# Pooled attention and two expert layers on one core: moving the keys, the second attention tile and the first weights to other places in a hand-written order

## The chip, the core and the metric

The kernel runs on one core of a Trainium2 chip. The core has engines that each work through their own instructions in order and wait for one another through semaphores: TensorE (PE) multiplies and transposes into PSUM, its weight loads (PEld) running beside the multiplications; VectorE (DVE) and ScalarE (ACT) read PSUM and SBUF; GpSimd (POOL) reads SBUF; SyncE (SP) and the others issue DMAs. The metric is device time in microseconds, lower is better; times are medians of several runs.

## The reference

```python
# q, k, v: batch 8, heads 8, sequence 576, head size 64
k_p = k.reshape(B, H, 72, 8, D).mean(axis=3)
v_p = v.reshape(B, H, 72, 8, D).mean(axis=3)
scores = (1 / sqrt(D)) * q @ k_p^T                  # 576 x 72 per head
attn = exp(scores - max); attn /= sum + 1e-9
x = (attn @ v_p)                                    # -> 4608 tokens x 512
h = x @ w_in; x = max(0.01 * h, h) @ w_out          # 512 -> 2048 -> 512, float64 weights
logits = x @ w_gate; e = argmax(logits)             # 8 experts, one per token
out = softmax(logits)[e] * (max(x @ w1[e], 0) @ w2[e])   # 512 -> 1024 -> 512
```

Keys and values are averaged over groups of 8 positions. All products are done with numbers split into a high and a low part (three multiplications for one).

## The kernel before

**Stages.** The 4608 tokens are 36 tiles of 128, two tiles to a block of 256, so 18 blocks. The first expert layer runs in 288 *slots*. A slot (b, f) is one `g1(b, f)` (12 multiplications of 256 columns: 512 inputs to 128 hidden units) and, one or two slots later, one `g2(b, f)` (6 multiplications of 512 columns, back to 512 outputs). Slots 0 to 31 hold blocks 0 and 1, interleaved; from slot 32 on a block b has the 16 slots 16b to 16b + 15. After slot 287 comes the second expert layer, which gathers tokens by expert.

**What is hung on the slots.** `at(slot, fn, ...)` puts a call into a list for a slot. In each slot the order is: `g1`, the calls of the list in the order in which they were put there (`run_slot`, line 956), `g2`, then the split of the hidden units (`g_hi`, `g_lo`). `plan()` (line 893) puts the calls there: first all attention calls, then `att_av`, then the keys and values, then the preparation of the second layer's weights (`ps_load`, `ps_split`, `ps_store`), then routing (`logit`, `route_a` to `route_c`). So in one slot attention stands ahead of keys and values, and these ahead of the logits.

**Attention of a tile t** of block b is done in the slots of block b - 1, counted from s: `att_a` (s - 1: four PE transposes of the queries, ScalarE copies them out), `att_b` (s + 1: scores into two PSUM banks; DVE takes the max and subtracts it, into `pr`, once per bank), `att_e` (s + 2: exp), `att_n` (s + 3: sum and normalisation on DVE), `att_c` (s + 5: PE transposes into two banks; ScalarE copies the high part to `at_t` and then `rm_t`, DVE subtracts to get the low part, into `at_t` and `rm_t`). `att_av(b)`, in the last slot of block b - 1, multiplies with the values: operands `at_t`, `rm_t`, `vm` (the first 64 pooled values of each head) and `vr` (the other 8). Its result `x_t` is the input of block b's `g1`.

**Keys and values of batch nb** (2 to 7): seven pieces of raw data, in two buffers (`kv`): 0 to 3 keys, 4 and 5 values, 6 the rest of the values. `kv_load` is a DMA on SP's queue. `kv_pool` adds up groups of 8, in three DVE additions (and a POOL multiplication, line 294, for piece 6), two slots ahead of `kv_use` (one for the pieces 4 to 6). `kv_use` of 0 to 3 is one PE transpose (line 307) and two ScalarE copies to `kT`; of 4 and 5 copies and subtractions to `vm`; of 6 the same to `vr`. `kv_load(i + 2)` follows `kv_use(i)`, as it takes its buffer.

**The PSUM banks.** Every PE result of attention, keys and routing takes one of two banks, in turn; a new one waits until the one before last is read:

```python
banks = {"att": ["a0", "a1"], "h": ["h0", "h1"]}
...
def pt(kind):
    turn[kind] += 1
    return bank(banks[kind][turn[kind] % len(banks[kind])])
...
        if i < 4:                                        # kv_use
            p = pt("att")
            nc.tensor.transpose(p[:, 0:SP], t[:, 0, 256:384], ident[0:SP, 0:SP])
```

**The start.** Before slot 0 a list written out by hand does batch 0's keys and values (`kv_load0_k`, `kv_load0_v`), the attention of tiles 0 and 1, and the first weights. The first layer's weights come as float64; `w_load64` loads a piece of 0.5 MB (`load2` calls it twice: a piece of `w_in` and one of `w_out`), `w_conv1` turns it into float32 (two ScalarE steps, lines 459 and 460, then four DVE instructions, lines 461 to 470), `w_conv2` splits it into high and low. The pieces 1 to 15 of both are converted in the slots.

Of the kernel before, what the change touches and what calls it, by code (L numbers as in the profile page):

```python
# [21 lines left out]
def kernel(  # L22
# [25 lines left out]
    NF = DFF // P  # L48
# [59 lines left out]
    def sb(shape, dt, tag, bufs=1):  # L108
        return pool.tile(shape, dt, name=tag, tag=tag, bufs=bufs)
# [7 lines left out]
# [3 lines that stand above are left out]
# [4 lines left out]
    def act_copy(o, i, scale=1.0):  # L124
        nc.scalar.activation(o, i, AF.Copy, scale=scale)  # L125

    def sub(eng, o, a, b):
        eng.tensor_tensor(out=o, in0=a, in1=b, op=ALU.subtract)  # L128
# [85 lines left out]
    def kv_load0_v(nb):  # L214
        vt = sb([P, 6, 512], F32, "w13")
        for par in range(2):
            nc.sync.dma_start(
                out=vt[64 * par:64 * par + 64, 0:4],
                in_=v[nb, par:H:2, 0:512, :].rearrange("h (m r) d -> m h (r d)", r=POOL),
            )  # L220
        for h in range(H):
            nc.sync.dma_start(
                out=vt[8 * h:8 * h + 8, 4, :], in_=v[nb, h, 512:576, :].rearrange("(m r) d -> m (r d)", r=POOL)
            )
        kv_raw[nb, 4] = vt[:, 0:2]
        kv_raw[nb, 5] = vt[:, 2:4]
        kv_raw[nb, 6] = vt[0:64, 4:5]
        kv_raw[nb, 7] = vt[0:64, 5, :].rearrange("p (h d) -> p h d", h=H)
# [107 lines left out]
    def segs(c0, n):  # L336
        r, done = [], 0
        while done < n:
            b, s = divmod(c0 + done, S)
            w = min(n - done, S - s)  # L340
            r.append((done, w, b, s))
            done += w
        return r

    def q_load(t):
        x = q0[:, t] if t < 4 else sb([P, H, D], F32, "q")
        for o, n, b, s in segs(t * P, P):
            nc.sync.dma_start(out=x[o:o + n], in_=q[b, :, s:s + n, :].rearrange("h s d -> s h d"))
        q_sb[t] = x

    def att_a(t):
        x = q_sb.pop(t)
        p = pt("att")
        for pr in range(NPAIR):
            nc.tensor.transpose(p[:, pr * P:pr * P + P], x[:, 2 * pr:2 * pr + 2, :], ident)
        qT = alt[:, 0:512].rearrange("p (a n) -> p a n", a=NPAIR) if t in (1, 3) else sb([P, NPAIR, P], F32, "qT")
        act_copy(qT, p.rearrange("p (a n) -> p a n", a=NPAIR))
        qT_sb[t] = qT

    def att_b(t):  # L360
        qT = qT_sb.pop(t)
        if t in (1, 3):
            pr_t = alt[:, 512:512 + H * SP].rearrange("p (h m) -> p h m", h=H)
            st = alt[:, 2048:2048 + 3 * H].rearrange("p (a h) -> p a h", a=3)
        else:
            pr_t = sb([P, H, SP], F32, "pr")
            st = sb([P, 3, H], F32, "st")
        half = H // 2
        for g in range(2):
            p = pt("att")  # L370
            for i in range(2):
                pr = 2 * g + i
                for o, n, b, _ in segs(t * P, P):
                    nc.tensor.matmul(
                        p[o:o + n, i * 2 * SP:(i + 1) * 2 * SP], qT[:, pr, o:o + n], kT[b % 2][:, pr, :],
                        start=True, stop=True,
                    )
            pv = p[:, 0:half * SP].rearrange("p (h m) -> p h m", h=half)
            hs = slice(half * g, half * g + half)
            nc.vector.tensor_reduce(st[:, 0, hs], pv, axis=AX.X, op=ALU.max)  # L380
            sub(nc.vector, pr_t[:, hs], pv, st[:, 0, hs].unsqueeze(2).to_broadcast([P, half, SP]))
        p_sb[t] = (pr_t, st)

    def att_e(t):
        pr_t = p_sb[t][0]
        nc.scalar.activation(pr_t, pr_t, AF.Exp)
# [65 lines left out]
    def w_conv1(kind, f):  # L452
        V = nc.vector
        r = w_raw.pop((kind, f))
        rw = r[:].bitcast(U32).rearrange("p (n t) -> p n t", t=2)
        lw, hw = rw[:, :, 0], rw[:, :, 1]
        h = r[:].bitcast(BF16).rearrange("p (n t) -> p n t", t=4)[:, :, 3]
        e = e_t[(2 * f + kind) % 2]
        nc.scalar.activation(ab_t, h, AF.Abs)
        nc.scalar.activation(e, ab_t[:].bitcast(U16), AF.Relu, scale=8.0 * 65536.0, bias=ebias)  # L460
        V.scalar_tensor_tensor(
            out=e, in0=hw, scalar=0x80000000, in1=e, op0=ALU.bitwise_and, op1=ALU.bitwise_or
        )
        V.tensor_scalar(
            out=hw, in0=hw, scalar1=3, scalar2=0x7FFFF8, op0=ALU.logical_shift_left, op1=ALU.bitwise_and
        )
        V.scalar_tensor_tensor(
            out=hw, in0=lw, scalar=29, in1=hw, op0=ALU.logical_shift_right, op1=ALU.bitwise_or
        )
        V.tensor_tensor(out=hw, in0=hw, in1=e, op=ALU.bitwise_or)  # L470
        w_mid[kind, f] = hw
# [418 lines left out]
    def at(slot, fn, *a):  # L890
        hooks.setdefault(slot, []).append((fn, a))

    def plan():
        for t in range(4, NT // P):
            b, i = divmod(t, TPB)
            s = (b - 1) * NF + 1 + 7 * i
            at(s - 1, att_a, t)
            if t + 1 < NT // P:
                at(s - 1, q_load, t + 1)
            at(s + 1, att_b, t)  # L900
            at(s + 2, att_e, t)
            at(s + 3, att_n, t)
            at(s + 5, att_c, t)
        for b in range(2, NB):
            at((b - 1) * NF + NF - 1, att_av, b)
        for nb in range(2, B):
            t = S * nb // P
            b, i = divmod(t, TPB)
            sb_ = (b - 1) * NF + 2 + 7 * i
            use = []  # L910
            c = sb_ - 1
            while len(use) < 4:
                if c % NF in (1, 3, 5, 8, 10, 12, 14) and (not use or use[0] - c >= 3):
                    use.insert(0, c)
                c -= 1
            use += [use[3] + 2, use[3] + 4, use[3] + 6]
            for i in range(7):
                at(use[i], kv_use, nb, i)
                if i + 2 < 7:
                    at(use[i], kv_load, nb, i + 2)  # L920
                at(use[i] - 2 + (i > 3), kv_pool, nb, i)
            at(max(use[0] - 6, 0), kv_load, nb, 0)
            at(use[0] - 5, kv_load, nb, 1)
        for i in range(E * NCH):
            s = 34 + i * 9 // 5
            at(s, ps_load, i)
            at(s + 2, ps_split, i)
            at(s + 3, ps_store, i)
        for b in range(NB - 1):
            s = (b + 1) * NF + 1  # L930
            lg_at = []
            if b == 0:
                at(30, y_evac, 0)
                at(31, y_tr, 0, 0)
                at(32, y_tr, 0, 1)
                at(33, y_logit, 0)
                r = (34, 36)
            elif b == 1:
                ev, r = 37, (46, 48)
                lg_at = [38 + j // 2 for j in range(16)]  # L940
            elif b == NB - 2:
                ev, r = None, (s + 9, s + 11)
                lg_at = [s + j // 2 for j in range(16)]
            else:
                ev, r = None, (s + 15, s + 19)
                lg_at = [s + max(j - 1, 0) for j in range(16)]
            if b == 1:
                at(ev, y_evac, b)
            for j, x in enumerate(lg_at):
                at(x, logit, b, j)  # L950
            at(r[0], route_a, b)
            at(r[1], route_b, b)
            at(r[1], route_c, b, 0)
            at(r[1] + 2, route_c, b, 1)
# [34 lines left out]
    with tc.manual_schedule():  # L989
# [19 lines left out]
        def load2():  # L1009
            for _ in range(2):  # L1010
                if w_todo:
                    w_load64()

        kv_load0_k(0)
        q_load(0)
        q_load(1)
        kv_load0_v(0)
        load2()
        load2()
        q_load(2)  # L1020
        q_load(3)
# [5 lines left out]
        consts1()  # L1027
        att_a(0)
        att_a(1)
        att_b(0)  # L1030
        att_e(0)
        kv_pool(0, 4, nc.gpsimd)
# [4 lines left out]
        att_n(1)  # L1037
        kv_pool(0, 6)
        att_c(0)
        w_conv1(0, 0)  # L1040
        kv_use(0, 4)
        kv_use(0, 5)
        att_c(1)
# [21 lines left out]
        at(27, gate_rows)  # L1065
        at(4, q_load, 4)
        plan()
        pend = []

# [49 lines left out]
        b = NB - 1  # L1119
# [101 lines left out]
```

## Time and profile before

| | |
|---|---|
| median of 3 runs | 1569.41 us (1565.23 to 1569.67) |
| the profiled execution | 1560.74 us, of which the span from first to last instruction 1559.0 us |
| mean granted clock of PE | 0.985 of full speed |
| busy, share of the span | PE 95%, PEld 83%, DVE 59%, ACT 41%, POOL 21% |

The profile shows one execution. Busy time counts instructions that run; register and DMA-issuing instructions aren't counted. An idle time that ends at an instruction is put down to the engine and instruction that released it.

### The profile page before, as it was taken

To read this page: it belongs to the slowest core of one execution; us is meant where nothing else is said; L and a number is where in the kernel's file an instruction comes from. 1 tells how busy PE (TensorE), PEld (TensorE's weight loads), DVE (VectorE), ACT (ScalarE), POOL (GpSimd) and SP (SyncE) were. 2 spreads that over 40 slices of the span, in tenths; PEclk is the share of its full clock that TensorE was granted. 3 is DMA by queue.
4 is the path that set the end of the run, shared out by engine and by line. 5 is a ranking of instruction groups with operands and counts; after the bars stand their busy time and mean duration, and the time that the engine had idled before them with its cause. 6 is when DMAs were issued, how large, how long until landed. Compare 5 with 4: busy or idle time off the path is not lost. (4 is left out here: it accounts for less than half of the span.)

```text
span 1559.0 us, 25084 instructions
## 1 busy us (share of the span) xinstructions
PE 1482.3 (95%) x8824; PEld 1296.9 (83%) x8824; DVE 920.3 (59%) x2371; ACT 643.8 (41%) x1442; POOL 327.6 (21%) x294
## 2 busy tenths in 40 slices
PE   4598999999999999999999999999999999999998
PEld 3476889899898898899999899977888888888886
DVE  6998768878878878877878887743111111111111
ACT  4676534544544454544444444322222222222222
POOL 4000012223232222222232233021111111111111
PEclk8799999999999999999999999999999999999999
DMA  9543135456445555545655454064721331661250
GB/s 213 148 134 100 73 127 166 158 198 186 159 150 195 171 183 159 186 154 178 176 167 189 140 181 153 17 238 168 299 84 41 149 147 41 248 264 47 67 231 22
DMA packets 121384, 238.01 MB, mean 153 GB/s; under 512 B 56845, under 2 KB 65041, under 8 KB 117544
## 3 DMA queue, kind: packets, MB, share of 16 engines
q1 hardware_dynamic: 90312, 139.81, 29.0%
q10 hardware_dynamic: 23328, 76.56, 12.9%
q0 software_dynamic: 7616, 20.01, 3.9%
q8 instruction: 71, 1.16, 0.3%
q14 instruction: 57, 0.47, 0.1%
HBM read 418.44 MB, written 87.38 MB: 324 GB/s over the span
## 5 line engine op out<-in xcount | busy, mean ns | idle before, releaser
L522 PE MATMUL y<-w,ghl 128*128 128x512 f32 x1728 | 461.2, 403 | 3.8 <-DVE ghl L128 3.7
L522 PEld LDWEIGHTS y<-w,ghl 128*128 128x128 f32 x1728 | 306.1, 189 | 62.0 <-DVE ghl L128 7.8
L128 POOL TENSOR_TENSOR ps<-ps 128x512 f32<-128x512 f32 x128 | 182.5, 1426 | 477.2 <-ACT ps L125 366.7
L494 PEld LDWEIGHTS h<-x_t,w 128*128 128x128 f32 x1776 | 238.2, 194 | 39.8 <-DVE w L128 18.2
L494 PE MATMUL h<-x_t,w 128*128 128x256 f32 x1776 | 245.7, 288 | 24.0 <-DVE w L128 16.8
L494 PEld LDWEIGHTS y<-x_t,w 128*128 128x128 f32 x1488 | 193.2, 189 | 9.7
L542 DVE CUSTOM_DVE_ANT_0 junk<-y,wg 128x512 bf16<-128x512 f32 x256 | 198.4, 775 | 1.9
L494 PE MATMUL y<-x_t,w 128*128 128x256 f32 x1488 | 196.0, 282 | 0.0
L128 DVE TENSOR_TENSOR at_t<-a,at_t 128x512 fp32r<-128x512 f32 x76 | 52.4, 689 | 203.3 <-ACT at_t L125 203.0
L128 DVE TENSOR_TENSOR vm<-a,vm 128x512 fp32r<-128x512 f32 x40 | 27.7, 692 | 199.3 <-ACT vm L125 199.3
L125 ACT ACTIVATE g<-h 128x256 f32<-128x256 f32 x164 | 62.8, 383 | 146.3 <-PE h L494 134.6
L866 PE MATMUL y<-w,at_t 128*128 128x512 f32 x480 | 120.9, 400 | 1.4 <-ACT at_t L125 0.9
L874 POOL DMA_INDIRECT out_dram<-kv,sidx x40 | 40.4, 1009 | 381.7 <-ACT vm L125 192.0
L866 PE MATMUL y<-w,vm 128*128 128x512 f32 x480 | 120.1, 399 | 0.0
L840 PE MATMUL h<-w,x_t 128*128 128x512 f32 x480 | 118.0, 394 | 0.0
L840 PE MATMUL y<-w,x_t 128*128 128x512 f32 x480 | 118.0, 395 | 0.0
L866 PEld LDWEIGHTS y<-w,at_t 128*128 128x128 f32 x480 | 88.8, 188 | 21.8 <-ACT at_t L125 1.2
L866 PEld LDWEIGHTS y<-w,vm 128*128 128x128 f32 x480 | 88.8, 188 | 19.8
L840 PEld LDWEIGHTS h<-w,x_t 128*128 128x128 f32 x480 | 88.6, 188 | 18.7 <-DVE x_t L128 0.4
L840 PEld LDWEIGHTS y<-w,x_t 128*128 128x128 f32 x480 | 88.6, 188 | 18.2
L502 DVE TENSOR_TENSOR h<-g,h 128x256 f32<-128x256 f32 x132 | 56.0, 424 | 77.9 <-ACT g L125 77.4
L125 ACT ACTIVATE ps<-ps 128x512 fp32r<-128x512 f32 x128 | 80.5, 629 | 21.6 <-DMA ps<-in_moe_w_dram 12.9
(254 smaller groups left out, 1900.8 us busy)
## 6 DMA issues: line engine op xcount, KB each, us to landing
w<-wsp SPq DMA_DIRECT2D x156, 2048.0 KB
wsp<-ps ACTq DMA_DIRECT2D x128, 512.0 KB
ps<-in_moe_w_dram SPq DMA_DIRECT2D x128, 256.0 KB
y_d<-y ACTq DMA_DIRECT2D x18, 512.0 KB
q<-in_q_dram SPq DMA_DIRECT2D x28, 256.0 KB
kv<-in_k_dram SPq DMA_DIRECT2D x24, 288.0 KB
kv<-in_v_dram SPq DMA_DIRECT2D x24, 256.0 KB
ps<-in_moe_w_in_dram SPq DMA_DIRECT2D x8, 512.0 KB
```

What stands on the lines that cost most here:

```text
L125: nc.scalar.activation(o, i, AF.Copy, scale=scale)
L128: eng.tensor_tensor(out=o, in0=a, in1=b, op=ALU.subtract)
L494: nc.tensor.matmul(p[:, 0:BLK], win(f)[:, kk, l], xv[:, kk, r], start=(n == 0), stop=(n == 3 * KD - 1))
L502: nc.vector.tensor_tensor(out=g, in0=t, in1=h, op=ALU.max)
L522: nc.tensor.matmul(y_ps[b, i], hl[:, l, i * P:i * P + P], wout(f)[:, r], start=(f == 0 and l + r == 0), stop=(last and l == 1),)
L542: nc.vector.tensor_tensor_reduce(out=jk, in0=y_sb[b][:, i], in1=wg_t[0][:, e], scale=1.0, scalar=0.0, op0=ALU.mult, op1=ALU.add, accum_out ...
L840: nc.tensor.matmul(p, xT2[:, t % 2, kk, l], wlane(lane(t), fh * KD + kk)[:, r], start=(n == 0), stop=(n == 3 * KD - 1))
L866: nc.tensor.matmul(p, d[:, kk, l], wlane(lane(t), 2 * KD + 4 * j + kk)[:, r], start=(j == 0 and n == 0), stop=(j == 1 and n == 11),)
L874: nc.gpsimd.indirect_dma_start(out=out, out_offset=bass.IndirectOffsetOnAxis(ap=sidx[:, t:t + 1], axis=0), in_=o, in_offset=None, bounds_c ...
```

## The change

Three things move; no instruction is added or taken away. First, the attention of the second tile of each block (from tile 5 on) is one slot later: its `att_a`, `att_b`, `att_e`, `att_n` and `att_c` go from the slots 7, 9, 10, 11 and 13 of the 16 to 8, 10, 11, 12 and 14; the query load of the next tile goes with `att_a`. Second, the search for the slots of the keys and values of batches 3 to 7 begins four slots sooner. Third, at the start the first two weight pieces are loaded ahead of batch 0's values instead of behind them, and the first `w_conv1` stands ahead of the first scores instead of behind `att_c(0)`.

```diff
@@ plan()
         for t in range(4, NT // P):
             b, i = divmod(t, TPB)
-            s = (b - 1) * NF + 1 + 7 * i
+            s = (b - 1) * NF + 1 + 8 * i
             at(s - 1, att_a, t)
             if t + 1 < NT // P:
                 at(s - 1, q_load, t + 1)
...
             sb_ = (b - 1) * NF + 2 + 7 * i
             use = []
-            c = sb_ - 1
+            c = sb_ - (1 if nb == 2 else 5)
             while len(use) < 4:
                 if c % NF in (1, 3, 5, 8, 10, 12, 14) and (not use or use[0] - c >= 3):
                     use.insert(0, c)
@@ the start
         kv_load0_k(0)
         q_load(0)
         q_load(1)
+        load2()
         kv_load0_v(0)
-        load2()
         load2()
         q_load(2)
         q_load(3)
...
         att_a(0)
         att_a(1)
+        w_conv1(0, 0)
         att_b(0)
         att_e(0)
         kv_pool(0, 4, nc.gpsimd)
...
         att_c(0)
-        w_conv1(0, 0)
         kv_use(0, 4)
```

Worked out from these lines, the slots of the seven `kv_use` calls of each batch are:

| batch | before | after |
|---|---|---|
| 2 | 46 49 53 56 58 60 62 | the same |
| 3 | 78 81 85 88 90 92 94 | 69 74 78 83 85 87 89 |
| 4 | 117 122 126 129 131 133 135 | 113 117 120 124 126 128 130 |
| 5 | 149 154 158 161 163 165 167 | 145 149 152 156 158 160 162 |
| 6 | 190 193 197 200 202 204 206 | 181 186 190 195 197 199 201 |
| 7 | 222 225 229 232 234 236 238 | 213 218 222 227 229 231 233 |

## Rows read from the trace of the kernel before

**Rows 1.** Stages: busy us (instructions) by engine, granted clock, DMA share, GB/s.
```profile
0.00:160.00 160.00, 107.86 (x581) 89.06 (x582) 137.56 (x268) 95.47 (x191) 15.95 (x39) 0.87 0.55 145
160.00:1040.00 880.00, 864.71 (x5768) 788.55 (x5767) 694.13 (x1927) 409.58 (x1004) 229.22 (x174) 1.00 0.50 161
```

**Rows 2.** Line 433 (`att_av`), PE idle before it: until what; us, times.
```profile
  DVE vr L128: 4.2, 4
```

**Rows 3.** Timeline of PE, first and last of those: start, us, instruction [idle before].
```profile
301.87 0.30 PE L433 MATMUL a<-rm_t,vr 128*128 128x128 f32 x1 [0.74 <-DVE vr L128]
...
886.97 0.27 PE L433 MATMUL a<-rm_t,vr 128*128 128x64 f32 x1 [1.13 <-DVE vr L128]
```

**Rows 4.** Groups by shape: `att_a`, count | busy us, mean ns | idle before.
```profile
L355 PE MATMUL a<-ident,q 128*128 128x128 f32 x128 | 19.5, 275 | 4.1 <-DVE at_t L128 4.1
```

**Rows 5.** Timeline of PE: waits at slots 23, 46 and 134.
```profile
164.00 0.66 PE L355 MATMUL a<-ident,q 128*128 128x128 f32 x4 [1.24 <-DVE at_t L128]
...
245.47 0.29 PE L307 MATMUL a<-ident,kv 72*128 72x72 f32 x1 [0.43 <-DVE at_t L128]
...
538.63 0.38 PE L412 MATMUL a<-ident,pn 128*32 128x128 f32 x2 [0.97 <-DVE rtmp L599]
```

**Rows 6.** Timeline of PE and DVE behind `att_c` of tiles 7, 15, 29.
```profile
241.96 1.64 PE L522 MATMUL y<-w,ghl 128*128 128x512 f32 x6
...
455.09 1.64 PE L522 MATMUL y<-w,ghl 128*128 128x512 f32 x6
455.78 0.69 DVE L128 TENSOR_TENSOR at_t<-a,at_t 128x512 fp32r<-128x512 f32 x1 [0.16 <-ACT at_t L125]
...
826.98 1.64 PE L522 MATMUL y<-w,ghl 128*128 128x512 f32 x6
828.27 0.68 DVE L128 TENSOR_TENSOR at_t<-a,at_t 128x512 fp32r<-128x512 f32 x1
```

**Rows 7.** Timeline of PE and DVE behind `att_b` of tiles 11 and 12.
```profile
336.52 1.65 PE L522 MATMUL y<-w,ghl 128*128 128x512 f32 x6
337.14 0.46 DVE L128 TENSOR_TENSOR pr<-a,st 128x288 f32<-128x288 f32 x1
...
368.68 0.46 DVE L128 TENSOR_TENSOR pr<-a,st 128x288 f32<-128x288 f32 x1
369.10 1.09 PE L522 MATMUL y<-w,ghl 128*128 128x512 f32 x4
```

**Rows 8.** Timeline of DVE: pooling of two pieces of keys.
```profile
357.71 2.43 DVE L291 TENSOR_TENSOR kv<-kv 72x512 f32<-72x512 f32 x3
...
371.19 1.46 DVE L291 TENSOR_TENSOR kv<-kv 72x512 f32<-72x512 f32 x3
```

**Rows 9.** Timeline of the start: ACT, DVE and POOL.
```profile
15.96 0.60 ACT L125 ACTIVATE w<-a 128x512 f32<-128x512 f32 x1 [0.26 <-PE a L355]
...
17.12 0.46 DVE L380 TENSOR_REDUCE st<-a 128x4 f32<-128x288 f32 x1 [4.33 <-PE a L374]
...
18.06 5.16 POOL L291 TENSOR_TENSOR w<-w 128x512 f32<-128x512 f32 x6 [1.66 <-DMA w<-in_v_dram]
...
26.30 0.66 ACT L459 ACTIVATE junk<-ps 128x512 bf16<-128x512 bf16 x1
...
27.62 1.29 ACT L125 ACTIVATE vm<-w 64x128 fp32r<-64x128 f32 x4
27.84 0.69 DVE L461 SCALAR_TENSOR_TENSOR e<-ps,e 128x512 uint32<-128x512 uint32 x1
...
29.75 0.69 DVE L470 TENSOR_TENSOR ps<-ps,e 128x512 uint32<-128x512 uint32 x1
```

**Rows 10.** Stretches of 10 us, columns as in the first group.
```profile
0.00:10.00 10.00, 0.73 (x2) 0.36 (x2) 2.78 (x8) 1.38 (x2) 3.86 (x23) 1.00 0.71 155
...
130.00:140.00 10.00, 6.57 (x33) 5.16 (x34) 6.97 (x14) 6.67 (x13) 0.00 (x0) 0.78 0.41 123
140.00:150.00 10.00, 8.98 (x54) 7.22 (x50) 9.72 (x22) 6.14 (x12) 0.00 (x0) 0.88 0.37 106
```

## The prediction

> **What bounds the kernel now.** The page comes first: TensorE (PE) is its busiest engine. Then a table of stages [rows 1]. In the first 160 us PE lacks 160 - 107.9 = 52.1 us while VectorE (DVE) is busy for 137.6: there DVE sets the pace. From 160 to 1040 us, where the reordered slots lie, PE lacks only 880 - 864.7 = 15.3 us; after that nothing moves. So the reorder can win at most some 15 us in its long stage, every microsecond of it a PE wait, and a new PE wait costs its full length, since PE works in order and has nothing else to do. So I listed every PE wait of the timeline, and for each call that changes slot I read what PE does right behind it and when the reader of its PSUM bank is done. A block of 16 slots takes (886.97 - 301.87) / 11 = 53.2 us [rows 3], a slot about 3.3.
>
> **Part 1: the waits that go.** At the end of a block `att_av` waits for `vr`, the last piece of the values, which `kv_use(6)` writes one slot ahead, in slot 14 of 16. Four such waits sum to 4.2 us [rows 2]. Batches 3, 6 and 7 now have `vr` in slot 9, six slots before its use; batch 2 keeps its slots and its 0.74 [rows 3]. Gain 4.2 - 0.74 = 3.46. `att_a` of the second tile stands one slot behind `att_c` of the first and takes the bank that `att_c` used, so it waits for DVE's subtraction into `at_t`: 4.1 us in all [rows 4], of which 1.24 at 164.00 [rows 5]. With one more slot between them that wait goes: 4.1 - 1.24 = 2.9. The 1.24 lies at the end of the stretch where DVE sets the pace, so part of it will only move: 0.5 (between 0 and 1.24). The 0.97 at 538.63 [rows 5] comes from a pooling of batch 4 between `att_n` and `route_b` in one slot; batch 4 is done by then now: 0.97. Sum of gains: 3.46 + 2.9 + 0.5 + 0.97 = 7.8 us.
>
> **Part 2: the waits that come.** All attention work shares two PSUM banks in turn, so each allocation waits for whoever reads the one before last. `att_b` and `att_c` take both banks; a `kv_use` of keys (0 to 3) is one PE transpose that takes one. Before, the key slots allowed (1, 3, 5, 8, 10, 12, 14 of 16) never met the second tile's 7, 9 and 13. Now that tile has 8, 10 and 14, and within a slot the attention call stands ahead of the key call. Three kinds of meeting follow.
> - Keys right behind `att_c` (slots 46, 78, 190, 222). PE must wait until DVE has subtracted into `at_t`. Three places price it, as the end of that subtraction, plus 0.06 for the signal, less the start of PE's next work [rows 6]: 828.27 + 0.68 + 0.06 - 826.98 = 2.03 for tile 29; 455.78 + 0.69 + 0.06 - 455.09 = 1.44 for tile 15, where DVE waited only for ScalarE; and tile 7, where DVE was behind, let a key transpose through at 245.47 [rows 5], 3.51 after 241.96. Slot 46 is tile 7's: block 1's logits run there two a slot, and `att_n` and a pooling now share slot 44. I take 3.2, less the 0.43 that it waits already [rows 5]: 2.8. For the other three 1.7, between tiles 15 and 29: 5.1.
> - Keys right behind `att_b` (slots 74, 186, 218). PE waits for DVE's max and subtraction on the first half. Tile 11: 337.14 + 0.46 + 0.06 - 336.52 = 1.14 [rows 7]. Three times: 3.4.
> - Keys one slot behind the first tile's `att_b` (slots 83, 195, 227). Today that subtraction for tile 12 ends at 369.14 and PE gets there at 369.10 [rows 7]: it just fits. But the pooling of those keys now stands in slot 1, ahead of `att_b` in DVE's queue, and takes 1.46 to 2.43 us [rows 8]. I take 1.2 each, as another pooling leaves the slots just before: 3.6 (between 1.4 and 6.5).
>
> Sum of losses: 2.8 + 5.1 + 3.4 + 3.6 = 14.9 us. Bounds: all at the undisturbed price, 1.0 + 4.3 + 3.4 + 1.4 = 10.1; with DVE everywhere as far behind as at tile 7, 3.1 + 10.5 + 9 + 6.5 = 29.
>
> The Trainium skill (Perfetto Trace Analysis, section Optimizing Tensor Performance) says that independent matmul groups should rotate through PSUM banks, so that the evacuation of one overlaps the next group's matmuls. The wait at 245.47 [rows 5] agrees; by that rule the key transposes right behind `att_c` speak against this change.
>
> **Part 3: the rest of the reorder, taken as nothing.** `att_c` of the second tile now stands one slot, not two, ahead of `att_av`. Behind its transposes PE has a `g2` and the next `g1` to do, some 2.9 us; undisturbed, DVE is done with `at_t` 1.44 us into that and has one half-size subtraction left. That is the cover; a DVE that is 1.5 us behind, as at tile 7, would cost about 0.5 a block, 8 over sixteen. In the three blocks where the late poolings held DVE up they are gone. SP's queue carries the same loads, in the same order among themselves; a key load still has three slots (10 us) to its pooling at the tightest, as before, and a query load eight slots where it had nine. What waits behind POOL's multiply for the last value piece is weight splits; the last of their stores is issued 17 slots ahead of the first read.
>
> **Part 4: the start.** `w_conv1(0, 0)` is four DVE instructions from 27.84 to 30.44, 2.6 us, in a stretch where DVE never rests [rows 9]. They go to where DVE idled 4.33 us until 17.12. But ScalarE must do its two steps first, and these now stand behind the copy that ends at 16.56; DVE followed their start by 27.84 - 26.30 = 1.54. So DVE starts at 18.1 and comes to `att_b(0)` at 20.7, 3.6 later, less the 2.6 saved: +1.0 us. The weights are issued at about 4 us. The first 10 us moved 155 GB/s [rows 10], 1.55 of the 1.7 MB of keys and queries that go ahead; 0.5 MB more is there by about 14.5, before 16.6. The values land some 5 us later; their pooling on POOL, 5.16 us, then ends near 28.3, and ScalarE reads them behind `att_c(0)`, at 27.62 today [rows 9], at some 31 then. Were the weights 2 us later, all of that would be added. Range 0 to +3.
>
> **Sum.** -7.8 + 14.9 + 1.0 = +8.1 us. The profiled execution took 1560.74 (span 1559.0 and 1.7 around it), so 1568.8; the runs' median lies 8.7 above it, and against that I predict 1577.5.
>
> **Rivals.**
> - *The new waits are cheap.* DVE keeps up and each meeting costs its undisturbed price; tile 5 gives its full 1.24: -8.5 + 10.1 + 1.0 = +2.6, so 1572.0, no change that can be told (0.3%, 4.7 us, is about what this measurement can tell). For it: some poolings move to emptier slots. Against it: tiles 7 and 29.
> - *The key transposes do not wait* (faster). If DVE is done before PE gets there, or the bank is handed on without it, the change only removes waits: -7.8 + 1.0 = -6.8, so 1562.6. It decides where the ten meetings wait less than 6.8 us together, 0.7 each. Against it: [rows 4] and the 0.43 at 245.47 are this very wait.
> - *PE's clock falls after the waits* (slower still). Where PE was busy for only 6.57 of 10 us, the granted clock was 0.78, and 0.88 in the next 10 [rows 10]: a part of these stretches at the 1.2 GHz level, which gives back 2.2 + 1.2 = 3.4 us of work at 2.4 GHz. From 160 to 1040 us it rounds to 1.00 [rows 1], through waits of up to 1.24. If the waits at slots 46, 83 and 227 near 3 us: three times 3.4, +10, so 1587.5. The Trainium skill (TensorE: Matmul & The Clock Gate, section HAM oscillation) has it that gaps between batches of matmuls bring the slow clock back; no steady slot of this trace shows it.
>
> **How the numbers follow.** Forecast 0.50, clock 0.12, cheap waits 0.25, no waits 0.13. So slower by over 0.3% has 0.62, within it 0.25, faster 0.13. The range leaves out the faster rival and the tail of the clock's: 1566 to 1589; the forecast's own is 1574 to 1585.
>
> **What would show it.** Right: waits on the key transposes (line 307) in ten slots, ended by DVE's `at_t` subtraction at slots 46, 78, 190 and 222 and by its `pr` subtraction at the other six; the waits on `vr` down to one; `att_a` never waiting on `at_t` past 160 us; DVE's first reduction near 20.7 and the first `g1` 1 us later. Wrong: no wait at line 307 over 0.5 us; `att_av` waiting on `rm_t` in most blocks (part 3's cover gone); `w_conv1(0, 0)` waiting for its DMA past 17 us; poolings that wait for loads.

## The result, and the profile after

The changed kernel takes 1590.02 us (median of 4 runs, 1588.67 to 1593.77) where the kernel before took 1569.54 (4 runs, 1565.23 to 1570.03): a ratio of 1.014, with a 95% interval of 1.0116 to 1.0165. It is slower, as forecast, but by 20.5 us where 8.1 were forecast, and 1.0 us outside the range. The profiled execution took 1589.81 us (span 1588.1), 29.1 more in span than the profiled execution of before, which itself lay 8.8 below the median of these runs; that distance comes up again below.

The stages of the changed kernel, columns as in [rows 1], to be read against those rows:

```profile
0.00:160.00 160.00, 111.74 (x576) 93.03 (x577) 134.98 (x264) 94.89 (x188) 16.14 (x39) 0.83 0.55 145
160.00:1040.00 880.00, 851.10 (x5637) 773.67 (x5636) 701.84 (x1871) 401.74 (x989) 222.77 (x168) 0.99 0.48 154
```

In the long stage PE lacks 880 - 851.1 = 28.9 us instead of 15.3, and the granted clock is no longer 1.00. What PE waited for there, by groups of instructions (count | busy us, mean ns | idle before, and until what):

```profile
L522 PE MATMUL y<-w,ghl 128*128 128x512 f32 x1541 | 412.5, 404 | 5.2 <-DVE ghl L128 3.4 <-ACT ghl L125 1.6
...
L355 PE MATMUL a<-ident,q 128*128 128x128 f32 x124 | 19.0, 277 | 0.0
...
L307 PE MATMUL a<-ident,kv 72*128 72x72 f32 x24 | 5.9, 247 | 19.6 <-DVE at_t L128 10.6 <-issue 7.3 <-PE a L374 1.7
L433 PE MATMUL a<-rm_t,vr 128*128 128x128 f32 x16 | 4.4, 278 | 0.3 <-DVE vr L128 0.3
```

`att_a` (line 355) has lost its waits [rows 4], `vr` all but 0.3 of its 4.2 [rows 2], and the key transposes (line 307) have gained 19.6. Line 522 (`g2`), which waited 0.1 in this stretch before, now waits 5.2: nothing in the prediction stands for that. The ten waits of line 307, from PE's timeline:

```profile
251.84 0.28 PE L307 MATMUL a<-ident,kv 72*128 72x72 f32 x1 [3.69 <-DVE at_t L128]
348.05 0.25 PE L307 MATMUL a<-ident,kv 72*128 72x72 f32 x1 [0.85 <-PE a L374]
362.67 0.38 PE L307 MATMUL a<-ident,kv 72*128 72x72 f32 x1 [2.32 <-DVE at_t L128]
384.32 0.25 PE L307 MATMUL a<-ident,kv 72*128 72x72 f32 x1 [2.43 <-issue]
727.84 0.25 PE L307 MATMUL a<-ident,kv 72*128 72x72 f32 x1 [1.07 <-issue]
742.43 0.28 PE L307 MATMUL a<-ident,kv 72*128 72x72 f32 x1 [2.31 <-DVE at_t L128]
761.58 0.25 PE L307 MATMUL a<-ident,kv 72*128 72x72 f32 x1 [1.33 <-issue]
838.80 0.25 PE L307 MATMUL a<-ident,kv 72*128 72x72 f32 x1 [0.85 <-PE a L374]
853.40 0.28 PE L307 MATMUL a<-ident,kv 72*128 72x72 f32 x1 [2.32 <-DVE at_t L128]
875.16 0.25 PE L307 MATMUL a<-ident,kv 72*128 72x72 f32 x1 [2.43 <-issue]
```

They stand in the ten slots that were named: 46, 74, 78, 83, 186, 190, 195, 218, 222 and 227. Six of the labels ("issue", "PE a L374") name no engine that reads PSUM. The timeline of GpSimd and VectorE ahead of the fourth wait (384.32) shows who it was:

```profile
380.85 1.29 POOL L128 TENSOR_TENSOR ps<-ps 128x512 f32<-128x512 f32 x1 [1.24 <-DMA ps<-in_moe_w_dram]
380.86 1.82 DVE L542 CUSTOM_DVE_ANT_0 junk<-y,wg 128x512 bf16<-128x512 f32 x1
...
383.28 0.44 DVE L380 TENSOR_REDUCE st<-a 128x4 f32<-128x288 f32 x1
383.76 0.46 DVE L128 TENSOR_TENSOR pr<-a,st 128x288 f32<-128x288 f32 x1
```

DVE's subtraction into `pr` on the first half of `att_b`'s scores ends at 383.76 + 0.46 = 384.22, and PE starts 0.10 later: the bank is what it waited for, though the label does not say so. Ahead of it in DVE's queue stands a logit (line 542) of 1.82 us; such a logit takes 0.68 when GpSimd is idle. It began 0.01 after a subtraction of GpSimd; an experiment below goes after that.

The clock, in windows of 5 us of the changed kernel around three of these waits:

```profile
360.00:365.00 5.00, 2.68 (x10) 1.99 (x8) 3.73 (x10) 2.21 (x7) 0.00 (x0) 0.74 0.24 83
365.00:370.00 5.00, 5.00 (x35) 4.65 (x34) 1.72 (x4) 2.17 (x5) 0.00 (x0) 0.92 0.76 183
385.00:390.00 5.00, 5.00 (x36) 4.53 (x35) 4.32 (x12) 2.70 (x7) 1.29 (x1) 1.00 0.80 224
...
740.00:745.00 5.00, 2.69 (x18) 2.30 (x17) 3.88 (x11) 3.22 (x9) 1.00 (x1) 1.00 0.30 94
745.00:750.00 5.00, 5.00 (x33) 4.51 (x33) 2.80 (x7) 1.96 (x4) 0.30 (x1) 1.00 0.94 273
```

With the wait at 362.67 the granted clock fell: a part of two windows is at the 1.2 GHz level, (0.26 + 0.08) x 5 = 1.7 us of work lost. Behind 251.84 and 853.40 it did the same. Behind 384.32 and 742.43, waits as long as the one at 362.67, it did not.

### The profile page after: what moved, and what is told of

Read it like the earlier page. It is cut to its first block, busy times and chain, and to the rows that moved or that the text cites. A ratio compares the mean times of both kernels' runs of the same rounds, so it can differ in the third digit from the quotient of the medians.

```text
span 1588.1 us, 25071 instructions
## 1 busy us (share of the span) xinstructions
PE 1498.3 (94%) x8824; PEld 1308.5 (82%) x8824; DVE 939.0 (59%) x2371; ACT 641.2 (40%) x1442; POOL 327.4 (21%) x294
## 5 line engine op out<-in xcount | busy, mean ns | idle before, releaser
L522 PE MATMUL y<-w,ghl 128*128 128x512 f32 x1728 | 468.1, 407 | 7.8 <-DVE ghl L128 6.1
L522 PEld LDWEIGHTS y<-w,ghl 128*128 128x128 f32 x1728 | 310.1, 192 | 68.5 <-DVE ghl L128 11.5
L494 PEld LDWEIGHTS h<-x_t,w 128*128 128x128 f32 x1776 | 243.3, 198 | 39.2 <-DVE w L128 17.2
L494 PE MATMUL h<-x_t,w 128*128 128x256 f32 x1776 | 250.2, 291 | 22.7 <-DVE w L128 15.4
L542 DVE CUSTOM_DVE_ANT_0 junk<-y,wg 128x512 bf16<-128x512 f32 x256 | 210.7, 823 | 1.8
L840 PEld LDWEIGHTS y<-w,x_t 128*128 128x128 f32 x480 | 88.6, 188 | 18.2
L125 ACT ACTIVATE ghl<-y 128x256 fp32r<-128x256 f32 x124 | 47.4, 382 | 125.2 <-DVE y L502 90.0
```

What stands on the lines that cost most here:

```text
L494: nc.tensor.matmul(p[:, 0:BLK], win(f)[:, kk, l], xv[:, kk, r], start=(n == 0), stop=(n == 3 * KD - 1))
L522: nc.tensor.matmul(y_ps[b, i], hl[:, l, i * P:i * P + P], wout(f)[:, r], start=(f == 0 and l + r == 0), stop=(last and l == 1),)
L542: nc.vector.tensor_tensor_reduce(out=jk, in0=y_sb[b][:, i], in1=wg_t[0][:, e], scale=1.0, scalar=0.0, op0=ALU.mult, op1=ALU.add, accum_out ...
L840: nc.tensor.matmul(p, xT2[:, t % 2, kk, l], wlane(lane(t), fh * KD + kk)[:, r], start=(n == 0), stop=(n == 3 * KD - 1))
```

## The experiments

Each kernel was timed in five rounds beside the kernel before on the same chip, but for the last, which ran once. The kernel before took 1566.94 us beside the first four, 1565.79 beside `free_slots`, `free_slots_no_start`, `own_bank_before` and `load_only`, and 1568.62 beside `behind_att_c`, `slot_three` and `free_slots_tile_before`, so kernels of different groups are compared by their ratios. Edits are against the changed kernel where nothing else is said. The theory: in this order of work a key transposition that meets an attention step waits for its PSUM bank, and these waits, with what follows from them, are the loss. The main rivals: keys and values come too soon for DVE and POOL; the later second tile costs by its own chain; the start costs more than a microsecond.

**One part at a time.** `tile_later` is the kernel before with the second tile alone a slot later:

```
-            s = (b - 1) * NF + 1 + 7 * i
+            s = (b - 1) * NF + 1 + 8 * i
```

> The kernel before with the first part alone (second tile one slot later; keys, values and start as before). Theory (a key transpose that stands in one slot with the second tile's attention waits for its PSUM bank): keys meet att_c in slots 46, 78, 126, 158, 190 and 222 (3.3 more at 46, 2.3 each at the others) and att_b in slots 122 and 154 (0.9 each), +16.6; the waits of att_a on at_t go, -2.9: about 1583. Rival (moving the keys sooner is what costs, by DVE's and the loads' times): nothing of that is here, so 1567 to 1570. Rival (the start costs most): 1567 to 1570 too.

`keys_sooner` is the kernel before with the keys and values alone moved:

```
-            c = sb_ - 1
+            c = sb_ - (1 if nb == 2 else 5)
```

> The kernel before with the second part alone (keys and values of batches 3 to 7 four slots sooner; second tile and start as before). Theory: no key transpose shares a slot with the second tile's attention, so only the three waits one slot behind the first tile's att_b stay (2.4, 1.3 and 2.4 us, +6.1), and the vr waits and the one of slot 134 go (-4.4): +1.7, about 1571, within 0.3%. Rival (sooner keys cost by themselves): most of the 20 us, above 1580.

`start_only` is the kernel before with `load2()` and `w_conv1(0, 0)` alone moved, as in the change:

> The kernel before with the third part alone (first weights loaded ahead of the values and converted ahead of the first scores). Theory: the first layer starts some 2 us later and stays so: 1571 to 1573, and the clock of the first 180 us a little lower. Rival (the start costs most of the 20 us, by the clock or by later loads): above 1580.

Measured: 1582.06 us, a ratio of 1.0102 (1.0082 to 1.0122); 1572.0, 1.0026 (1.0008 to 1.0045); 1570.06, 1.0016 (1.0000 to 1.0033). The product is 1.0144, the whole change 1.014. Alone, the tile's move costs most; but the parts do not meet in the same slots alone as together (their waits below sum to 23.2, those of the changed kernel to 19.6), so that the product fits is partly chance. The waits on line 307, first of `tile_later`, then of `keys_sooner`:

```profile
L307 PE MATMUL a<-ident,kv 72*128 72x72 f32 x24 | 6.0, 252 | 16.6 <-DVE at_t L128 14.8 <-PE a L374 1.8
```

```profile
L307 PE MATMUL a<-ident,kv 72*128 72x72 f32 x24 | 5.6, 232 | 6.6 <-issue 6.2 <-DVE at_t L128 0.4
```

Each part alone already brings key waits: the later tile meets the keys in their old slots (the sum of 16.6 was the expected one), the sooner keys come into slot 3.

**The bank taken away.** `own_bank` gives the key transposes of batches 2 to 7 a PSUM bank of their own, taken from the four banks of `h`:

```
-    banks = {"att": ["a0", "a1"], "h": ["h0", "h1"]}
+    banks = {"att": ["a0", "a1"], "h": ["h0", "h1"], "key": ["y3"]}
...
-            p = pt("att")
+            p = pt("key" if nb > 1 else "att")
...
-                banks["h"] += ["y2", "y3"]
+                banks["h"] += ["y2"]
+            if (b, f) == (16, 0):
+                banks["h"] += ["y3"]
```

> The changed kernel, but the key transposes of batches 2 to 7 get a PSUM bank of their own (y3), which the hidden layer's banks lack until slot 256. Order and work are those of the changed kernel. Theory: the ten waits at line 307 (19.6 us in the changed kernel's profile) go and with them the clock's drops behind them (some 5 us): about 1566, at or below the kernel before. Rival (poolings and loads come at the wrong time for DVE, or the start costs): it stays at 1585 to 1590.

`own_bank_before` does the same to the kernel before:

> The kernel before, with the key transposes in a bank of their own, taken from the banks of the transposes of h (three until slot 256 where there were four): the control of own_bank. Before has one wait on line 307, 0.43, so the bank itself brings nothing here. Theory (own_bank stayed above before because three h banks bring waits on the transposes of h, some 4.4 at two places): 2 to 6 above before, a ratio of 1.001 to 1.004, and own_bank against it is then no more than 1.001. Rival (three banks cost nothing, own_bank's rest is the start and the knock-on waits of the change): within 1 of before, a ratio below 1.001.

`own_bank` took 1573.6 us, 1.0039 (1.0022 to 1.0057). That is a miss: the waits on line 307 went from 19.6 to 0, but 1566 was expected. In their place `g2` waits 8.2 us from 160 to 1040 us (5.2 in the changed kernel), and `g1` waits for its banks. `own_bank_before` took 1575.12, 1.0055 (1.0034 to 1.0075): the third bank of `h` alone costs the kernel before 0.55%, more than the 2 to 6 us expected. Against that control the change has a ratio of 1.0039 / 1.0055 = 0.998: with the bank out of the way it is no longer slower by what these intervals can tell. In the traces `g1` waits 2.1 us in this stretch before, 6.6 in `own_bank_before` and 7.3 in `own_bank`. Two groups of `own_bank`, the key transposes and the larger of the two groups of `g1`:

```profile
L494 PE MATMUL h<-x_t,w 128*128 128x256 f32 x1992 | 265.8, 283 | 5.0 <-DVE ghl L128 4.2 <-DVE w L128 0.8
...
L307 PE MATMUL y<-ident,kv 72*128 72x72 f32 x24 | 5.5, 227 | 0.0
```

**The meetings taken away.** `free_slots` keeps all banks and the whole change, and lets keys stand only where they meet no attention step:

```
-                if c % NF in (1, 3, 5, 8, 10, 12, 14) and (not use or use[0] - c >= 3):
+                if c % NF in (1, 5, 9, 12) and (not use or use[0] - c >= 3):
```

> The changed kernel with one number list altered: key calls may stand in slots 1, 5, 9 and 12 of a block, so that none shares a slot with the second tile's steps (8, 10, 14) and none stands in slot 3. Theory (a key transposition waits only because it stands in a slot right behind an attention step or the tail of one, whose scores still occupy one of the two attention banks): none of the ten waits on line 307 is left, those summing to 19.6 in the profile; with the clock that hung on three of them the time falls by 16 to 22, to about 1567 to 1574, a ratio of 0.999 to 1.005. Rival 1 (being four slots sooner is itself what costs: the values' part, or the poolings, come too soon for DVE and POOL): the waits move to other slots and the time stays above 1582. Rival 2 (the second tile one slot later is what costs, by its own chain): stays near 1582, as with the second tile moved alone.

`free_slots_no_start` also undoes the start:

> The same slots (1, 5, 9, 12) in the changed kernel, and the part at the start undone: load order and first conversion of weights as before the change. Theory: with the key waits gone, what is left of the change is the 7.8 of waits that it removes, against some 4 to 5 of short waits that tile_later and own_bank also showed on the transposes of h and on one att_av: 1563 to 1569, a ratio of 0.997 to 1.001, and 2 to 3 below free_slots, since the part at the start measured 1.0016 by itself. Rival (the start's part is hidden behind the other waits once they are gone): equal to free_slots within 1.

1560.72 us, 0.9962 (0.9947 to 0.9977), and 1558.38, 0.9955 (0.9938 to 0.9972). Both are faster than the kernel before, and one list of numbers makes 1.8% between `free_slots` and the changed kernel. Both moves are still in `free_slots`, so neither the sooner keys nor the later tile is by itself what costs: it is where they meet. By the ratio both came out below what was expected, by 0.3% and 0.15%, but 2.3 us apart, as expected; the second is the best kernel of this study. Line 307 of `free_slots`:

```profile
L307 PE MATMUL a<-ident,kv 72*128 72x72 f32 x24 | 5.4, 227 | 0.0
```

**One kind of meeting put back.** `behind_att_c` allows slot 14 again, (1, 5, 9, 12, 14), so that four keys stand right behind `att_c`; `slot_three` allows slot 3, (1, 3, 5, 9, 12), so that three stand one slot behind `att_b`.

> free_slots with slot 14 allowed again (1, 5, 9, 12, 14): one key call each in slots 46, 78, 190 and 222 stands right behind att_c of the second tile; no other key call meets an attention step, none is in slot 3. Theory (each meeting costs its wait, and where TensorE stands for 2.3 or more the granted clock then falls for some us): the four waits of the changed kernel come back, 3.7 and three times 2.3, 10.6 in all, with 2 to 6 for the clock: 13 to 17 above free_slots, 1573 to 1578, a ratio of 1.004 to 1.008. Rival (the clock's part in the changed kernel was not due to these waits): 10 to 11 above free_slots, near 1571, with no window of PEclk below 0.95 behind them.

> free_slots with slot 3 allowed again (1, 3, 5, 9, 12): the fourth key call of three batches stands in slots 83, 195 and 227, right behind att_b of the first tile in slot 2, as in the changed kernel and in keys_sooner; the values of these batches are two slots later than in free_slots. Theory: waits of 2.4, 1.3 and 2.4 come back, 6.2 in all, without a fall of the clock, since none stood behind the ones of the changed kernel: 5 to 8 above free_slots, 1566 to 1569, a ratio of 1.000 to 1.002. Rival (the third key call, no longer in slot 10, leaves the fourth enough room: the bank is free): within 2 of free_slots.

`behind_att_c`: 1578.26 us, 1.0051 (1.0028 to 1.0074), against 0.9962 some 14 us more. `slot_three`: 1569.9, 0.9991 (0.9970 to 1.0012), some 4.5 more, a little under the 5 to 8 expected; the waits themselves came back (6.2 us on line 307). The kinds cost different amounts, as the theory has it. Line 307 and five windows of `behind_att_c`:

```profile
L307 PE MATMUL a<-ident,kv 72*128 72x72 f32 x24 | 6.0, 248 | 12.4 <-DVE at_t L128 12.4
```

```profile
250.00:255.00 5.00, 2.27 (x6) 1.89 (x7) 4.56 (x18) 2.95 (x9) 0.60 (x1) 0.55 0.23 23
250.50:252.70 2.20, 0.00 (x0) 0.00 (x0) 2.14 (x7) 1.42 (x5) 0.00 (x0) 0.51 0.00 0
255.00:260.00 5.00, 5.00 (x32) 4.77 (x32) 2.31 (x7) 1.47 (x4) 0.70 (x1) 0.76 0.53 193
...
735.00:740.00 5.00, 2.68 (x13) 2.02 (x12) 3.99 (x12) 2.84 (x8) 0.50 (x1) 0.86 0.19 72
740.00:745.00 5.00, 5.00 (x32) 4.82 (x32) 1.54 (x3) 1.80 (x4) 0.77 (x1) 0.80 0.79 190
```

With the first wait (4.43 here, until 252.73) the clock was lower for (0.45 + 0.24) x 5 = 3.5 us' worth; but it fell during the wait, and in 2.2 us of it (second row) PE had nothing to do, so 3.5 - 0.49 x 2.2 = 2.4 us of work were lost. The wait of 2.32 before 737.93 is followed by 1.7 lost; at its twin in the changed kernel (742.43) nothing was. In `slot_three` the clock fell behind two of the three waits, against its expectation that none would. So waits of 2.3 to 2.4 us bring a fall in some executions and none in others.

**The keys alone in free slots.** `free_slots_tile_before` is the kernel before with the keys four slots sooner and slot 3 struck out:

```
-            c = sb_ - 1
+            c = sb_ - (1 if nb == 2 else 5)
...
-                if c % NF in (1, 3, 5, 8, 10, 12, 14) and (not use or use[0] - c >= 3):
+                if c % NF in (1, 5, 8, 10, 12, 14) and (not use or use[0] - c >= 3):
```

> The kernel before with the keys alone moved, four slots sooner and out of slot 3 (slots 1, 5, 8, 10, 12, 14); second tile and start as before the change. Theory (the second tile one slot later is worth the 2.9 of waits of att_a behind the transposed weights, the keys sooner the 3.5 of vr waits, less some 3 of new ones on ghl): no wait on line 307 above 0.5, att_a waits as in keys_sooner (some 4.4), 1561 to 1565, a ratio of 0.998 to 1.000, 3 to 5 above free_slots_no_start. Rival (the tile's move is worth nothing by itself): equal to free_slots_no_start within 1.5.

1565.23 us, 0.9969 (0.9947 to 0.9990). By its ratio it was faster than expected, and its interval overlaps that of `free_slots_no_start` (0.9955): whether the tile's move is worth anything once the keys are out of its way can't be told by the times. In the traces, from 160 to 1040 us, it takes away the 6.4 us that `att_a` waits here and adds 1.7 to the waits of `g2` (3.4 here, 5.1 there). Moving the keys alone does gain: the interval lies below 1.

**The load at the start.** `load_only` is the kernel before with `load2()` alone ahead of the first values:

> The kernel before with only the load order at the start altered: the load of the second set of weights ahead of the first values. The conversion of the first weights stays behind the first att_c. Theory (the start's 2 us come from the conversion on VectorE ahead of the first reduction): no change against before, within 1, first reduction as before. Rival (the values arrive later behind the weights, and the first pooling of values with them): 1 to 2 longer, with the whole of the offset that start_only showed by 210 us.

1566.41 us, 1.0006 (0.9987 to 1.0026): no change that can be told. In its trace the `g2` that starts at 150.06 in the kernel before starts at 150.57, in `start_only` at 152.16: up to there most of the start's cost comes with the conversion. By 210 us the trace is 1.9 late all the same, as the rival has it; 1.4 of that came after 164 us, where a fall of the clock stands (0.66 in the window 165 to 170 us) that the kernel before has at 155 to 160. The interval of the time is too wide to tell 1 or 2 us from none, so the rival is made unlikely here, not excluded.

**The long logits.** `pool_away` moves three of GpSimd's 128 subtractions behind the logit that each preceded by a moment:

```
+            late = 2 if i in (26, 88, 106) else 0
-            at(s + 2, ps_split, i)
-            at(s + 3, ps_store, i)
+            at(s + 2 + late, ps_split, i)
+            at(s + 3 + late, ps_store, i)
```

> The changed kernel with three of the 128 weight splits of the second layer (pieces 26, 88, 106) and their stores two slots later: GpSimd's subtraction of each, which in the changed kernel begins just ahead of a logit of VectorE (line 542) in the slot before 83, 195 and 227, then runs behind it. Theory (that logit took 1.82, 1.66 and 1.82 instead of 0.68 because GpSimd's subtraction held VectorE, and the key transpose in slot 3 waits longer by the same amount): the three logits take 0.68 again and the waits of line 307 in slots 83, 195 and 227 fall from 2.43, 1.33 and 2.43 to near 1.3, 0.3 and 1.3, the sum on line 307 from 19.6 to about 16.4; the time falls by 3, within what one run shows. Rival (VectorE is late for its own queue of work, and GpSimd's subtraction stands there by chance): the waits stay within 0.3 of what they were.

One run, 1586.56 us, which a single run can't tell from the changed kernel. Its timeline can: one of the three logits, and the three waits.

```profile
379.63 0.69 DVE L542 CUSTOM_DVE_ANT_0 junk<-y,wg 128x512 bf16<-128x512 f32 x1
...
381.95 0.25 PE L307 MATMUL a<-ident,kv 72*128 72x72 f32 x1 [1.29 <-issue]
...
759.46 0.25 PE L307 MATMUL a<-ident,kv 72*128 72x72 f32 x1 [0.36 <-PE h L494]
...
873.88 0.25 PE L307 MATMUL a<-ident,kv 72*128 72x72 f32 x1 [1.31 <-issue]
```

2.43, 1.33 and 2.43 became 1.29, 0.36 and 1.31, to within 0.1 of what was expected, and all three logits took 0.69. GpSimd's subtraction did hold VectorE. The time it cost is another matter: line 307 waits 16.2 us instead of 19.6, but `g2` waits 8.7 instead of 5.2, and the first layer ends at 1051.54 where it ended at 1051.96. In this one execution the waits went elsewhere; that the hold itself cost the kernel time is not shown.

## Why the prediction was right about the sign and wrong about the size

The first layer ends, for this purpose, where PE begins to wait for the first gathered tokens (line 645). The table takes that time against the kernel before (1025.64 us) and sets beside it three things read from each trace: how late the `g1` is that starts at 210.40 before (what the start and tile 5 did), by how much PE's waits from there to 1020 us differ from the 10.0 of before, and the work lost in 5 us windows with a granted clock below 0.97 (0 in the profiled execution of before; in `behind_att_c` less the 1.1 that fell on the wait itself).

```
                     layer 1 later   at 210 us   PE waits   clock   sum of the three
changed kernel           +26.3         +3.1       +16.6      5.1        24.8
tile_later               +18.1         +0.6       +11.3      5.1        16.9
keys_sooner               +6.7         -0.4        +5.8      0.0         5.4
start_only                +9.5         +2.1        -0.6      8.5        10.0
own_bank                 +15.1         +3.0        +4.7      3.3        11.0
own_bank_before          +10.6         -0.2        +5.7      5.1        10.6
behind_att_c             +19.1         +3.1        +7.2      7.5        17.8
slot_three                +9.3         +3.2        +2.7      3.4         9.2
free_slots                +0.7         +3.2        -4.2      0.0        -1.0
free_slots_no_start       -0.5         +1.2        -4.1      0.0        -2.9
free_slots_tile_before    +6.1         -0.2        +1.0      3.4         4.2
load_only                 +8.1         +1.9        +3.0      3.4         8.3
pool_away                +25.9         +3.2       +15.2      3.4        21.8
```

The three account for it to within 2.4 us, except in `own_bank` and `pool_away`, where 4.1 stay open in each. Against the changed kernel's +26.3 the forecast of +8.1 is 18.2 too little (the other 2.8 of the 29.1 by which the spans differ come after the first layer): the ten key waits were 4.3 longer, `g2` and one `att_av` waited 5.3 that were taken as nothing, the waits on `vr` fell by 0.5 more than forecast, the start with tile 5 cost 2.6 more, the clock 5.1 that the sum left to a rival, and 1.5 stay open. Now the prediction's own terms.

**Part 1, the waits that go: right.** 7.8 was forecast. After 210 us 3.95 of the `vr` waits, 2.9 of `att_a`'s and the 0.97 are gone, 7.8. That the sum agrees so well is luck: the 0.5 for tile 5 was wrong (`tile_later` and `free_slots_no_start` come to the `g1` at 210 us 0.6 and 1.2 later, not sooner), and batch 2's wait on `vr`, 0.74, which was to stay, fell to 0.3.

**Part 2, the waits that come: all ten places right, the sizes too small.** With the 0.43 of before, 15.3 was forecast and 19.6 measured. Behind `att_c` 3.2 became 3.69, and 1.7 became 2.32, 2.31 and 2.32: together 2.3 too little. Tiles 15 and 29 [rows 6] were too cheap a measure: at slot 78 the transposes of `att_c` are done and PE idle from 360.35, but DVE still has logits and products of line 502 to work off, from 359.29 on, and its subtraction into `at_t` begins at 361.92. ScalarE's copy, which the subtraction needs too, is no sooner: ScalarE had waited for DVE until 360.74.

```profile
360.74 0.39 ACT L125 ACTIVATE ghl<-y 128x256 fp32r<-128x256 f32 x1 [2.95 <-DVE y L502]
...
361.28 0.60 ACT L125 ACTIVATE at_t<-a 128x512 fp32r<-128x512 f32 x1
361.51 0.41 DVE L502 TENSOR_TENSOR y<-g,y 128x256 f32<-128x256 f32 x1
...
361.92 0.69 DVE L128 TENSOR_TENSOR at_t<-a,at_t 128x512 fp32r<-128x512 f32 x1
```

The price is DVE's queue in the new slot, directly and by way of ScalarE, not the subtraction. Behind `att_b` 1.14 became 0.85, 1.07 and 0.85, 0.6 too much. In slot 3, 1.2 became 2.43, 1.33 and 2.43, 2.6 too little, and `pool_away` shows why: without GpSimd's hold on DVE they are 1.29, 0.36 and 1.31, 3.0 where 3.6 was forecast. There DVE's own queue was costed well in sum; that another engine stands in it was not seen. It could be read in the trace of before, a little ahead of tile 12's subtraction [rows 7]:

```profile
365.77 1.29 POOL L128 TENSOR_TENSOR ps<-ps 128x512 f32<-128x512 f32 x1 [6.23 <-ACT ps L125]
365.80 1.81 DVE L542 CUSTOM_DVE_ANT_0 junk<-y,wg 128x512 bf16<-128x512 f32 x1
```

**Part 3, the rest of the reorder, taken as nothing: this step failed.** In the long stage of the changed kernel `g2` waits 5.2 us for the split of the hidden units where it waited 0.1, and one `att_av` waits 0.9 for `at_t` (that cover held in the other blocks; the case of 0.5 a block did not come). Of the 5.2, 2.7 is there with the keys alone moved and 3.6 with the tile alone: what was moved puts more DVE work between a `g1` and its split, in slots that the argument did not look at (the longest of these waits, 1.20 at 655.16, stands behind 1.59 us of subtractions into `vr` and a logit). `free_slots` has 5.0 too. With the undersized waits of part 2 this is about half of the miss; most of the rest is the start and the clock.

**Part 4, the start: +1.0 forecast, some 2 measured.** At the `g2` that waits 0.79 us at 150.06 in the kernel before, the kernels with the start's part are between 152.07 and 152.31 (152.16 in the changed kernel and `start_only`), those without it between 149.67 and 150.57. `free_slots` less `free_slots_no_start` is 2.3 us in time. Timelines of ScalarE and VectorE, first of before, then of the changed kernel:

```profile
30.20 1.72 ACT L125 ACTIVATE vr<-w 32x256 fp32r<-32x256 f32 x4
...
36.82 1.28 DVE L128 TENSOR_TENSOR x_t<-a,x_t 128x512 fp32r<-128x512 f32 x2
```

```profile
20.41 0.45 DVE L380 TENSOR_REDUCE st<-a 128x4 f32<-128x288 f32 x1
...
32.63 1.72 ACT L125 ACTIVATE vr<-w 32x256 fp32r<-32x256 f32 x4
33.17 0.42 DVE L128 TENSOR_TENSOR vr<-w,vr 32x256 fp32r<-32x256 f32 x1
34.38 0.42 DVE L128 TENSOR_TENSOR vr<-w,vr 32x256 fp32r<-32x256 f32 x1 [0.80 <-ACT vr L125]
...
36.44 0.69 DVE L461 SCALAR_TENSOR_TENSOR e<-ps,e 128x512 uint32<-128x512 uint32 x1 [0.66 <-ACT e L460]
...
38.96 1.28 DVE L128 TENSOR_TENSOR x_t<-a,x_t 128x512 fp32r<-128x512 f32 x2
```

The first reduction came at 20.41 (20.7 forecast), and with the conversion out of its way DVE was back within 0.4 us by 33.17. But ScalarE, which waits for `att_b` and the transposes, came to `vr` 2.4 later, and DVE then waited for it (0.80, 0.66, and 0.29 between): `x_t` is 2.1 late. The +1.0 was made on DVE's work alone. The loads were not what cost: ScalarE began on the weights at 16.44, with no wait, and GpSimd on the values at 20.15, 2.1 later than before [rows 9] where some 5 was forecast.

**The rivals.** That the key transposes don't wait was wrong, and so were the cheap waits. The clock came true in part: 5.1 us in the changed kernel where the rival had 10, at 1.7 each, behind the waits of slots 46, 78 and 222 and not behind those of 83 and 227 that were named. The time of 1590.02 lies nearest to that rival's 1587.5 (chance 0.12), but half of its price isn't there: the number fits by terms that the rival did not have. Yet the clock does not simply add to the forecast, because the order of before has such falls too, though not in the profiled execution of before. `start_only` has the slots of before; its wait on `vr` and the windows behind it:

```profile
303.99 0.30 PE L433 MATMUL a<-rm_t,vr 128*128 128x128 f32 x1 [0.74 <-DVE vr L128]
```

```profile
305.00:310.00 5.00, 5.00 (x24) 4.52 (x24) 2.84 (x8) 1.82 (x3) 0.82 (x1) 0.60 0.14 57
310.00:315.00 5.00, 5.00 (x26) 4.28 (x25) 0.52 (x2) 0.90 (x3) 0.85 (x1) 0.72 0.00 0
```

A part of both windows is at the 1.2 GHz level. The same wait of 0.74 at 301.87 [rows 3] is followed, in the profiled execution of before, by this:

```profile
305.00:310.00 5.00, 5.00 (x31) 4.41 (x30) 2.02 (x6) 2.27 (x5) 1.68 (x1) 1.00 0.00 0
```

So 3.4 us were lost in the one and none in the other. In `start_only` it is 8.5 from 210 us on, about the 8.8 by which the median of before lies above its profiled execution (5 to 8 beside the experiments). That the two are the same thing is argued, not shown, but the spread of the runs speaks for it: beside `free_slots` the kernel before ran between 1561.19 and 1573.51 (28 runs) and `load_only`, which has its slots, between 1561.57 and 1575.39 (12 runs), `free_slots` between 1557.58 and 1562.10 (12 runs). The table speaks for it too: `load_only` and `own_bank_before` have falls, `free_slots` and `free_slots_no_start` none. It would also explain why `free_slots` came out below its expectation, and faster than before although its profiled execution is 1.3 us longer than that of before: removing a wait removes its falls of the clock, which the profiled execution of before had not shown to be there. The Trainium skill (TensorE: Matmul & The Clock Gate, section A second HAM failure mode: psum-queue depth-cycling) tells of a kernel that cycles through PSUM banks, whose TensorE idles briefly between groups of matmuls often enough for the clock to go back and forth; these rows agree, with falls behind waits as short as 0.74 us, and add that the same wait may or may not bring one.

## What to carry to other kernels

When a call moves in a hand-written order, list the buffer it takes (here one of two PSUM banks) and who holds it in the new slot: a reader on a busy engine makes the wait as long as that engine's queue, 0.9 to 3.7 us a meeting here. Price such a wait from a place with the same queue ahead of the reader, not from the nearest similar instruction, and look for the moves of all other work on that engine that the new order brings. Before giving a shared resource another unit, look for free slots: a bank for the keys, taken from `g1`, cost the kernel before 0.55%; a shorter list of slots gained 1.8% over the changed kernel.

## What the runs showed of the hardware

- A VectorE operation that reads two operands from SBUF (the logit: `y` and `wg`) can be held until a GpSimd operation ends. All 27 logits of the changed kernel that took more than 1.2 us began while GpSimd was running; none of the 141 that met an idle GpSimd took so long. Of the 115 that met a busy one 88 stayed under that: 65 of them had begun before GpSimd's operation, and the other 23 met only its last 0.57 us or less, met its DMA issue (line 609), or began within 0.01 us of it. The Trainium skill (SBUF — State Buffer, section SBUF: two separate sides) says that the two engines share a pair of ports as an exclusive lock, which goes to whichever of the two operations starts first; `pool_away` agrees, 1.82 against 0.69 us, and so do the 65. Ten of the 27 agree less well: they began during such a DMA issue, ahead of the subtraction that followed it, and yet ended only after it; why stays open.
- The granted clock of TensorE can fall to the 1.2 GHz level at waits of 0.74 to 4.4 us, in the midst of a stretch that is busy otherwise, at a loss of 1.7 to 3.4 us of work each time, and need not fall at the same wait in another execution. A profiled execution without such falls is a low base to predict from.
